# Seven MLP chunks in the partial sum, a tail in quadrants of 112 columns, and the first MLP weights on 112 rows, in a one-token transformer block

## The chip, the cores and the metric

The kernel runs on one core of a Trainium2 chip. The metric is the device time of one execution in microseconds (us). Before the change it is 213.39 us, the median of three runs (213.22 to 213.51).

## What is computed

One decode step of a transformer block for B = 4 tokens of width D = 448: attention over the last 1024 cached positions (16 query heads on 8 cached heads of 256), then a two-layer MLP of width F = 1792, each behind a layer norm, with residuals.

```python
h  = x + attention(layernorm(x), k_cache[:, :, 3072:], v_cache[:, :, 3072:]) @ wo
h2 = h + gelu(layernorm(h) @ w1 + b1) @ w2 + b2
```

All numbers are 32-bit floats. The kernel loads 88.30 MB, nearly all of it keys and values.

## The kernel before, in words

The host packs all inputs into a row of arrays, most of them 128 rows high, and SyncE (SP) loads them in one queue in the order of their use (`load`, L54): `wq0` and `k0`, the arrays `l1` to `l8` of about 8 MB each, then the last pieces `vo`, `v7`, `wo`, `w1`, `w2`. They go into three big SBUF buffers in turn (`slot`, L51), so SP waits until TensorE (PE) is done with an older array before it issues a new one. Each load is shared by 16 DMA engines. PE, SP and ScalarE (ACT) follow the order in which the code is written; VectorE (DVE) and GpSimd (POOL) are ordered by the compiler.

The change lies in the end of the kernel, from the last attention output on. There the batch is folded into **quadrants**: the 128 partitions are four groups of 32, the four tokens stand in the first rows of each group, and group j holds the j-th part of the 448 columns. A row of results is so 128 columns long and not 448. 448 is not four times 128: before the change, the first three quadrants hold 128 columns each, and the fourth holds the last 64 columns twice (`columns`, L235), so that each copy can be turned into 64 rows.

- `accs` (L425) is the output projection so far, all 448 columns. `add_quadrants` (L263) folds it with four matmuls into `last` (L430), and `add_rows` (L437) adds the rest of the projection.
- `h` to `hb` (L462 to L484) are the residual and the layer norm on [128, 128]. `fold` (L111) has a weight of 0.5/D in the fourth quadrant, because its columns count double. `zT` (L481) is the normed row turned by 90 degrees: three chunks of 128 rows, and a fourth that holds the 64 last rows twice.
- `pu` (L489, matmuls in L502) is the first MLP product, `zT` times `w1t`. `w1` is loaded in two DMAs (L402) on 128 rows: chunks 0 and 1 and the half-wide chunk 3 (rows 0 to 63 hold its left half, rows 64 to 127 its right half), then chunk 2. The loop (L498) goes 0, 1, 3, 2; for chunk 3 a matmul uses 64 rows (`w1_part`, L447). In each chunk four matmuls write the four quadrants of `pu`.
- `u` (L508) is GELU of it, `gT` and `gT_last` (L518, L522) hold it turned, as 14 chunks of 128 rows.
- The second product uses `w2`, which is loaded behind `w1` in five DMAs (L403): chunks 0 to 3, 4 to 7, 8 to 10, 11 and 12, and 13. Chunks 0 to 7 (`first = 8`) go into `pa` (L529), one matmul of 448 columns each, on quadrant c % 4. ACT copies `pa` to `pas` (L533). Chunks 8 to 13 go straight into `py` (L540), four matmuls each, one per quadrant. Behind chunk 10, `add_quadrants` adds `pas` to `py`.
- `res` (L546) is `py` plus `hb`; the last DMA stores it (L547).

`keep_warm` (L267) are matmuls on zeros that keep PE's clock up; they compute nothing.

Of the kernel before, what the change touches and what calls it, by code (L numbers as in the profile page):

```python
# [8 lines left out]
F32 = mybir.dt.float32  # L9
BF16 = mybir.dt.bfloat16  # L10
AF = mybir.ActivationFunctionType
ALU = mybir.AluOpType
# [3 lines left out]
B, D = 4, 448  # L16
# [3 lines left out]
F = 1792  # L20
P = 128
H = P // 2
ND = 4
NKC = W // P
NFC = F // P
FQ = F // 4
Q = 32
CACHE = NKC * B * DH
HALF = CACHE // 2
WEIGHTS = 4 * D  # L30
SLOT = CACHE + 2 * WEIGHTS + HALF
COLUMNS = ND * B + 4 + 4 * 4
EPS = 1e-5
SCALE = DH ** -0.5

# [1 line left out]
def block_kernel(ctx: ExitStack, tc, wq0, k0, wq1, l1, l2, l3, l4, l5, l6, l7, l8, vo, v7, wo, w1, w2, out):  # L37
    nc = tc.nc
    const = ctx.enter_context(tc.tile_pool(name="const", bufs=1))
    ring = ctx.enter_context(tc.tile_pool(name="ring", bufs=3))  # L40
    work = ctx.enter_context(tc.tile_pool(name="work", bufs=2))
    once = ctx.enter_context(tc.tile_pool(name="once", bufs=1))
    ps_s = ctx.enter_context(tc.tile_pool(name="ps_s", bufs=2, space=PSUM))
    ps_t = ctx.enter_context(tc.tile_pool(name="ps_t", bufs=2, space=PSUM))
    ps_o = ctx.enter_context(tc.tile_pool(name="ps_o", bufs=1, space=PSUM))
# [5 lines left out]
    def slot(name):  # L51
        return ring.tile([P, SLOT], F32, tag="r", name=name)

    def load(t, at, src, pieces=None):  # L54
        dst = t[:, at : at + src.shape[-1]]
        at = 0
        for n in pieces or (src.shape[-1],):
            nc.sync.dma_start(dst[:, at : at + n], src[:, at : at + n])  # L58
            at += n
        return dst  # L60

    def cut(t, sizes):
        parts, at = [], 0
        for n in sizes:
            parts.append(t[:, at : at + n])
            at += n
        return parts


    def wq_parts(y, t, last=None):  # L70
        parts = [(a, y[:, a, :], slice(0, 512), t[:, a * 512 : (a + 1) * 512]) for a in range(3)]
        if last is not None:
            return parts + [(3, y[:H, 3, :], slice(0, 512), last)]
        for i in range(2):
            parts.append((3, y[:, 3 + i, :], slice(i * 2 * P, (i + 1) * 2 * P), t[:, 3 * 512 :]))
        return parts
# [9 lines left out]
    def output_weights(t):  # L86
        return t.rearrange("p (j e) -> p j e", j=4)
# [9 lines left out]
    sel = const.tile([P, Q], F32, name="sel")  # L97
# [9 lines left out]
    zT = const.tile([P, ND, Q], F32, name="zT")  # L107
# [2 lines left out]

    fold = const.tile([P, 4, Q], F32, name="fold")  # L111
    for j in range(4):
        nc.vector.tensor_scalar_mul(fold[: 3 * Q, j, :], sel[: 3 * Q, :], 1.0 / D)
        nc.vector.tensor_scalar_mul(fold[3 * Q :, j, :], sel[3 * Q :, :], 0.5 / D)
    fold = fold.rearrange("p j q -> p (j q)")
    rows_of = ident.rearrange("p (j q) -> p j q", j=4)[:, :, :B]
    qT = [const.tile([P, 2, B, Q], F32, name=f"qT{i}") for i in range(2)]
    pT = [const.tile([P, NKC // 2, B, Q], F32, name=f"pT{i}") for i in range(2)]
    oT = [const.tile([P, 4, Q], F32, name=f"oT{i}") for i in range(2)]
    gT = const.tile([P, 12, Q], F32, name="gT")  # L120
    gT_last = const.tile([P, 2, Q], F32, name="gT_last")
    idle = const.tile([P, 512], BF16, name="idle")
    nc.vector.memset(idle, 0.0)
    for t in qT + oT + pT + [gT, gT_last]:
        nc.gpsimd.memset(t, 0.0)

    rs = const.tile([P, 2 * P + FQ], F32, name="rs")
    xb, b2b, b1b = rs[:, :P], rs[:, P : 2 * P], rs[:, 2 * P :]


    def column_mean(t, name):
# [46 lines left out]
    def score_tiles(n):  # L178
        return [ps_s.tile([P, 512], F32, tag="s", name=f"s{n}_{h}") for h in range(2)]
# [53 lines left out]


    def columns(t, j):  # L235
        if j < 3:
            return t[:, j * P : (j + 1) * P].rearrange("p (i c) -> p i c", i=2)
        return t[:, None, 3 * P :].to_broadcast([t.shape[0], 2, H])


    def transposed_output(n, po, rec, groups):
# [35 lines left out]


    t = slot("t0")
    wqt, xT, b2T, b1T = cut(load(t, 0, wq0), (WEIGHTS, ND * B, 4, 4 * 4))  # L280
    wqt = wq_parts(yT[0], wqt)
    xT = xT.rearrange("p (a b) -> p a b", a=ND)
    ka, kb, wqt1, k2 = cut(load(t, WEIGHTS + COLUMNS, k0), (HALF, HALF, 3 * 512, HALF))
    for i in range(2):
        nc.sync.dma_start(  # L285
            wq1_last[i * Q : (i + 1) * Q, :], wq1[i].rearrange("e (p c) -> e p c", c=512)[:, :4, :]
        )
    d = work.tile([P, ND, B], F32, tag="d", name="d_x")
# [10 lines left out]

    wide = once.tile([P, 2 * 512], F32, tag="p", name="wide")[:, : 6 * P].rearrange("p (n j q) -> p n j q", n=6, j=4)  # L300
    nc.vector.tensor_copy(
        wide[:, 0].rearrange("p j (r b) -> p j r b", b=B), xT[:, :, None, :].to_broadcast([P, ND, Q // B, B])
    )
    biases = b1T.rearrange("p (c j) -> p c j", j=4)
    nc.vector.tensor_copy(wide[:, 1], b2T[:, :, None].to_broadcast([P, 4, Q]))
# [10 lines left out]
    s = score_tiles(0)  # L316
# [16 lines left out]
    k2, v, wo_a, wo_b = cut(load(slot("l1"), 0, l1), (HALF, CACHE, WEIGHTS, WEIGHTS))  # L333
    scores(s, 1, 1, keys(k2))
    p, rec = softmax(0, s)
# [5 lines left out]
    v, wq_a, wq_b, ka = cut(load(slot("l2"), 0, l2), (CACHE, WEIGHTS, WEIGHTS, HALF))  # L341
# [3 lines left out]
    s = score_tiles(1)  # L345
# [7 lines left out]
    p, rec = softmax(1, s)  # L353
# [4 lines left out]
    v, va, wo_a, wo_b = cut(load(slot("l4"), 0, l4), (CACHE, HALF, WEIGHTS, WEIGHTS))  # L358
# [7 lines left out]
    s = score_tiles(2)  # L366
# [8 lines left out]
    p, rec = softmax(2, s)  # L375
# [6 lines left out]
    vb, v, k2 = cut(load(slot("l7"), 0, l7), (HALF, CACHE, HALF // 2))  # L382
    values(0, chunks(va) + chunks(vb), po, range(2, 4))
    values(1, chunks(v), po)
    s = score_tiles(3)
# [9 lines left out]
    e = [slot(f"te{i}") for i in range(3)]  # L395
    v, wot = cut(load(e[0], 0, vo), (CACHE, 2 * D))
# [2 lines left out]
    rest, wo_last = cut(load(e[0], CACHE + 2 * D, wo), (2 * D, WEIGHTS))  # L399
    wot, rest = (t.rearrange("p (j e) -> p j e", j=2) for t in (wot, rest))  # L400
    wo_last = output_weights(wo_last)
    w1t = cut(load(e[2], 0, w1, (2 * F + F // 2, F)), (F, F, F // 2, F))  # L402
    w2t = cut(load(e[1], CACHE, w2, (4 * D, 4 * D, 3 * D, 2 * D, D)), NFC * (D,))  # L403
    for h in range(2):
        scores(s, 1, h, kt[h])
    p, rec = softmax(3, s)
# [20 lines left out]

    keep_warm(3, warm)
    values(1, vt_last, po_last, alone=True)
    last = ps_s.tile([P, 512], F32, tag="s", name="last")[:, :P]  # L430
    ph = last.rearrange("p (i c) -> p i c", i=2)
    add_quadrants(ph, accs, True)
    keep_warm(1, warm)
    transposed_output(4, po_last, rec, range(1, 2))
# [9 lines left out]
        add_rows(oT[1], wo_last[:, i, :], i, i == 3)  # L444


    def w1_part(a, j):  # L447
        if a < 3:
            return slice(0, P), w1t[3 if a == 2 else a][:, FQ * j : FQ * (j + 1)]
        rows = slice(H * (j // 2), H * (j // 2) + H)  # L450
        return rows, w1t[2][rows, FQ * (j % 2) : FQ * (j % 2 + 1)]


    def row_mean(sums, at, name):
        nc.tensor.matmul(at, fold, sums, start=True, stop=True)
        return at
# [2 lines left out]
        return once.tile([P, 1], F32, tag=name, name=name)  # L459

    keep_warm(1, warm)
    h = once.tile([P, P], F32, tag="h", name="h")  # L462
    hs, ds = stat("hs"), stat("ds")
    squares = once.tile([P, 2], F32, tag="squares", name="squares")
    nc.vector.scalar_tensor_tensor(h, last, 1.0, xb, op0=ALU.mult, op1=ALU.add, accum_out=hs)
    pm = ps_m.tile([P, 2], F32, tag="m", name="pm")
    m = row_mean(hs, pm[:, 0:1], "m")
    keep_warm(2, warm)
    d = once.tile([P, P], F32, tag="dh", name="dh")
    nc.vector.tensor_scalar(d, h, m, None, op0=ALU.subtract, op1=ALU.add, accum_out=ds)  # L470
    pm2 = ps_m.tile([P, 2], F32, tag="m", name="pm2")
    m = row_mean(ds, pm2[:, 0:1], "m2")
    keep_warm(2, warm)
    z = once.tile([P, P], F32, tag="z", name="z")
    nc.vector.tensor_scalar(z, d, m, None, op0=ALU.subtract)
    junk = once.tile([P, P], F32, tag="junk", name="junk")
    nc.scalar.activation(junk, d, AF.Square, accum_out=squares[:, 0:1])
    nc.scalar.activation(junk, z, AF.Square, accum_out=squares[:, 1:2])
    pz = ps_m.tile([P, 4, B], F32, tag="m", name="pz")
    nc.tensor.matmul(pz, z, rows_of, start=True, stop=True)  # L480
    nc.vector.tensor_copy(zT[:, :, :B], pz)  # L481
    hb = once.tile([P, P], F32, tag="hb", name="hb")
    nc.vector.tensor_add(hb, h, b2b)
    keep_warm(2, warm)  # L484

# [1 line left out]
    s = stat("r2")  # L487
    u = once.tile([P, FQ], F32, tag="u", name="u")
    pu = ps_s.tile([P, 512], F32, tag="s", name="pu")[:, :FQ]  # L489
# [5 lines left out]
    rsqrt(s, v2, "r2")  # L495
    nc.vector.tensor_mul(s, s, r1)
    keep_warm(1, warm)
    for a in (0, 1, 3, 2):  # L498
        m = Q if a == 0 else B
        for j in range(4):  # L500
            rows, w = w1_part(a, j)
            nc.tensor.matmul(  # L502
                pu[j * Q : j * Q + m, :], zT[rows, a, :m], w, start=(a == 0), stop=(a == 2),
            )


# [11 lines left out]
    dst = gT.rearrange("p (c j) q -> p c j q", c=3)  # L518
# [3 lines left out]
        nc.scalar.copy(gT_last[rows, :, :B], put_last[rows].rearrange("p (j i) q -> p j i q", i=2)[:, :, i, :])  # L522
    keep_warm(1, warm)

    first = 8
    pa = ps_w.tile([P, D], F32, tag="acc", name="pa")
    for c in range(first):
        j, m = c % 4, Q if c < 4 else B
# [2 lines left out]
        )  # L531
    pas = once.tile([P, D], F32, tag="u", name="pas")
    nc.scalar.copy(pas, pa)  # L533
    py = ps_o.tile([P, 2, H], F32, tag="o", name="py")
    for c in range(first, NFC):
        g = gT[:, c, :] if c < 12 else gT_last[:, c - 12, :]
        for j in range(4):
            m, n = (Q, 2) if c == first else (B, 2 if j < 3 else 1)
            w = columns(w2t[c], j) if n == 2 else w2t[c][:, None, 3 * P :]
            nc.tensor.matmul(  # L540
                py[j * Q : j * Q + m, :n, :], g[:, :m], w, start=(c == first), stop=(c == NFC - 1),
            )
        if c == first + 2:
            add_quadrants(py, pas, False)
    res = once.tile([P, P], F32, tag="res", name="res")
    nc.vector.tensor_add(res, py.rearrange("p i c -> p (i c)"), hb)  # L546
    nc.sync.dma_start(out, res)  # L547


# [77 lines left out]
```

## Time and profile before

| | us |
|---|---|
| median of the runs | 213.39 |
| the profiled execution | 213.37 |
| its span, first to last instruction | 211.6 |
| time outside the span | 1.8 |
| PE busy | 134.4 |
| DVE busy | 27.4 |
| ACT busy | 14.3 |
| POOL busy | 5.0 |
| loaded | 88.30 MB |
| mean rate over the span | 418 GB/s |

The profile's times count from the start of the span. In a timeline a row has the start, the length, the engine, the line, the operation, output<-input, the size and the count; in brackets stands how long the engine had been idle before, and what ended the wait. PEld is PE's loading of weights, which runs beside its matmuls and shows most directly when a matmul's data were there. Several instructions of a kind are merged into one row. `te<-w` is a load of a piece of `w1` or `w2`.

### The profile page before, as it was taken

What the parts mean: (1) busy time and instruction counts of PE and PEld (TensorE: products, weight loads), DVE (VectorE), ACT (ScalarE), POOL (GpSimd) and SP (SyncE); (2) the same over time, 40 slices, a digit from 0 to 9 for tenths busy, and PEclk for the clock granted to TensorE, in tenths of its full rate; (3) what the DMA queues carried; (4) which work ended last, traced back from release to release, by engine and by line L of the source; (5) the groups of instructions that cost most, each with busy time, mean ns of one, the idle gap of its engine ahead of it and who ended that gap; (6) DMA issues with size and microseconds to landing.
All of it is one profiled execution on the core that took longest, in us unless ns stands there. A gap on an engine that the chain in (4) does not pass through costs nothing.

```text
span 211.6 us, 2239 instructions
## 1 busy us (share of the span) xinstructions
PE 134.4 (64%) x976; PEld 46.7 (22%) x976; DVE 27.4 (13%) x135; ACT 14.3 (7%) x34; POOL 5.0 (2%) x17
## 2 busy tenths in 40 slices
PE   0460787369058809844900892397299898888993
PEld 0330021022013302231200220123022332324332
DVE  1510011030001200320000110033002003103210
ACT  2010100020001000200000000012000002010311
POOL 5100000000000000000000000000000000000200
PEclk9999999787859985997975599589979999999999
DMA  8898988999899999999999998999999998999991
GB/s 344 355 481 373 563 384 384 420 540 389 384 444 492 408 387 456 468 408 396 471 444 420 408 516 384 395 469 412 455 412 455 409 440 387 426 401 446 411 409 68
DMA packets 3256, 88.42 MB, mean 418 GB/s; under 512 B 368, under 2 KB 624, under 8 KB 1456
## 3 DMA queue, kind: packets, MB, share of 16 engines
q1 hardware_dynamic: 3248, 88.30, 97.1%
q8 instruction: 7, 0.11, 0.2%
q14 instruction: 1, 0.01, 0.0%
HBM read 88.23 MB, written 0.07 MB: 417 GB/s over the span
## 4 chain that ended last, share of the span: by engine, by line
DMA 73%; PE 19%; another core or an unknown queue 3%; DVE 1%; SPq 1%; ACT 1%; issue 1%; ACTq 0%
DMA l<-l 51%; DMA te<-w 13%; PE po L226 10%; DMA te<-vo 9%; PE s L184 4%; PE acc L257 2%; PE py L540 1%; PE pq L153 1%; PE ppt L212 1%; SPq L285 1%; PE between L269 0%; ACT p L198 0%; SPq L58 0%; DVE mx L192 0%
## 5 line engine op out<-in xcount | busy, mean ns | idle before, releaser
L226 PE MATMUL po<-l,pT 128*32 128x512 f32 x192 | 30.0, 782 | 27.1 <-DMA l<-l 26.9
L184 PE MATMUL s<-l,qT 128*32 128x512 f32 x208 | 30.2, 726 | 18.1 <-DMA l<-l 18.1
L226 PEld LDWEIGHTS po<-l,pT 128*32 128x32 f32 x192 | 7.0, 136 | 46.4 <-issue 24.8
L184 PEld LDWEIGHTS s<-l,qT 128*32 128x32 f32 x208 | 7.3, 130 | 39.2 <-DMA l<-l 20.5
L198 ACT ACTIVATE p<-s,nm 128x512 f32<-128x512 f32 x8 | 5.4, 682 | 123.6 <-DVE nm L194 123.6
L192 DVE TENSOR_REDUCE mx<-s 128x1 f32<-128x512 f32 x8 | 5.5, 691 | 60.8 <-PE s L184 60.8
L243 DVE TENSOR_SCALAR o<-po,rec 128x512 f32<-128x512 f32 x5 | 3.8, 751 | 69.8 <-PE po L226 69.8
L269 PE MATMUL between<-idle 128*32 128x512 bf16 x48 | 11.5, 379 | 0.4 <-DVE pT L218 0.4
L153 PE MATMUL pq<-t,yT 128*32 128x512 f32 (+1 forms) x16 | 3.9, 951 | 9.8 <-DMA t<-k 7.0
L269 PEld LDWEIGHTS <-idle 128*32 128x32 bf16 x70 | 6.4, 96 | 10.9 <-issue 5.7
L184 PE MATMUL s<-t,qT 128*32 128x512 f32 x48 | 7.9, 824 | 0.7 <-DVE qT L176 0.7
L226 PE MATMUL po<-te,pT 128*32 128x512 f32 x64 | 7.3, 595 | 1.0 <-DMA te<-vo 0.8
L269 PE MATMUL warm<-idle 128*32 128x512 bf16 x22 | 6.8, 382 | 0.0
L212 PE MATMUL ppt<-ident,p 128*128 128x128 f32 x32 | 4.9, 288 | 2.2 <-ACT p L198 2.2
L257 PE MATMUL acc<-l,oT 128*32 128x448 f32 x48 | 5.1, 545 | 1.6 <-DVE oT L253 1.6
L167 PE MATMUL pqt<-ident,qs 128*128 128x128 f32 x16 | 3.1, 323 | 4.1 <-ACT qs L163 4.1
L153 PE MATMUL pq<-l,yT 128*32 128x512 f32 (+1 forms) x60 | 5.7, 507 | 0.0
L148 POOL TENSOR_TENSOR r<-ve_r,mhalf 128x1 f32<-128x1 f32 x2 | 1.1, 544 | 188.9 <-DVE ve_r L147 188.9
L212 PEld LDWEIGHTS ppt<-ident,p 128*128 128x128 f32 x32 | 3.5, 143 | 5.0 <-ACT p L198 5.0
L163 ACT COPY qs<-pq 128x512 f32<-128x512 f32 x4 | 2.3, 583 | 31.3 <-PE pq L153 31.3
L133 PE MATMUL pm_x<-t,mean 128*128 128x12 f32 x2 | 0.6, 364 | 5.5 <-DMA t<-wq 5.5
L218 DVE COPY pT<-ppt 128x16 f32<-128x16 f32 x32 | 3.4, 164 | 3.6 <-PE ppt L212 3.6
(115 smaller groups left out, 75.4 us busy)
## 6 DMA issues: line engine op xcount, KB each, us to landing
l<-l SPq DMA_DIRECT2D x6, 7936.0 KB, 43.3
l<-l SPq DMA_DIRECT2D x2, 7168.0 KB
t<-k SPq DMA_DIRECT2D x1, 6912.0 KB, 20.6
te<-vo SPq DMA_DIRECT2D x1, 4544.0 KB, 19.7
te<-v SPq DMA_DIRECT2D x1, 3072.0 KB, 24.3
te<-w SPq DMA_DIRECT2D x3, 896.0 KB, 22.9
te<-w SPq DMA_DIRECT2D x1, 2240.0 KB, 21.2
te<-wo SPq DMA_DIRECT2D x1, 1344.0 KB, 29.1
```

The source lines that it names most:

```text
L153: nc.tensor.matmul(pq[j * Q : (j + 1) * Q, cols], y, w, start=start and cols.start == 0, stop=not start and cols.stop == 512,)
L163: nc.scalar.copy(qs, pq)
L167: nc.tensor.transpose(pt[:, i, :], qs[:, i * P : (i + 1) * P], ident)
L184: nc.tensor.matmul(s[h][b * Q : (b + 1) * Q, :], qT[g][:, c, b, :], kt[:, c - cs.start, b, :], start=(g == 0 and c == 0), stop=(g == 1 and ...
L192: nc.vector.reduce_max(mx[:, h : h + 1], s[h], axis=AX.X)
L198: nc.scalar.activation(p[:, h * 512 : (h + 1) * 512], s[h], AF.Exp, bias=nm, scale=SCALE, accum_out=sums[:, h : h + 1],)
L212: nc.tensor.transpose(pt[:, c, :], p[:, (4 * h + c) * P : (4 * h + c + 1) * P], ident)
L218: nc.vector.tensor_copy(pT[g][:, 2 * h : 2 * h + 2, :, at : at + REP], src[:, :, i, :, 2 * g * REP : (2 * g + 1) * REP],)
L226: nc.tensor.matmul(po[b * Q : (b + 1) * Q], pT[g][:, c, b, :], vt[c][:, :, b, :], start=(c == 0 and (alone or g == 0)), stop=(c == NKC // ...
L243: nc.vector.tensor_scalar_mul(o, po, rec)
L257: nc.tensor.matmul(acc[i * Q : (i + 1) * Q, :], oT[g][:, i, :], wt[:, i, :], start=(n == 0 and g == 0), stop=(n == 3 if i < 2 else n == 2 ...
L269: nc.tensor.matmul(warm[:Q], idle[:, :Q], idle, start=True, stop=True)
```

## The change

The fourfold split of the 448 columns becomes even: each quadrant holds R = 112 columns, none of them twice. `columns` is a plain slice, and all tiles of the tail are [128, 112]. `fold` is 1/D everywhere. `zT` has four chunks of 112 rows. `w1` is packed by the host as four chunks of 112 rows, so that the load writes 112 partitions with rows of 7,168 floats, and not 128 partitions with rows of 6,272; the number of bytes is the same. Its first DMA takes three chunks (5,376 floats of each row, before 4,480), the second the fourth chunk. The half-wide chunk is gone.

In the second MLP product, seven chunks go into `pa`; chunk 7 goes into `py` with the rest, and `add_quadrants` stands right behind chunk 7.

Smaller things: `wq0` gets 16 more columns (x once more, in the new split), which is 8 KB. The output stays [128, 128]; `res` is now a constant tile that POOL clears at the start, and only 112 of its columns are written.

```diff
-COLUMNS = ND * B + 4 + 4 * 4
+R = D // 4
+COLUMNS = 2 * ND * B + 4 + 4 * 4
...
-    dst = t[:, at : at + src.shape[-1]]
+    dst = t[: src.shape[0], at : at + src.shape[-1]]
...
-    nc.vector.tensor_scalar_mul(fold[: 3 * Q, j, :], sel[: 3 * Q, :], 1.0 / D)
-    nc.vector.tensor_scalar_mul(fold[3 * Q :, j, :], sel[3 * Q :, :], 0.5 / D)
+    nc.vector.tensor_scalar_mul(fold[:, j, :], sel, 1.0 / D)
...
-    for t in qT + oT + pT + [gT, gT_last]:
+    res = const.tile([P, P], F32, name="res")
+    for t in qT + oT + pT + [gT, gT_last, res]:
         nc.gpsimd.memset(t, 0.0)
...
     def columns(t, j):
-        if j < 3:
-            return t[:, j * P : (j + 1) * P].rearrange("p (i c) -> p i c", i=2)
-        return t[:, None, 3 * P :].to_broadcast([t.shape[0], 2, H])
+        return t[:, j * R : (j + 1) * R]
...
-    w1t = cut(load(e[2], 0, w1, (2 * F + F // 2, F)), (F, F, F // 2, F))
+    w1t = cut(load(e[2], 0, w1, (3 * F, F)), 4 * (F,))
...
-    for a in (0, 1, 3, 2):
+    for a in range(ND):
         m = Q if a == 0 else B
         for j in range(4):
-            rows, w = w1_part(a, j)
             nc.tensor.matmul(
-                pu[j * Q : j * Q + m, :], zT[rows, a, :m], w, start=(a == 0), stop=(a == 2),
+                pu[j * Q : j * Q + m, :], zT[:R, a, :m], w1t[a][:R, FQ * j : FQ * (j + 1)],
+                start=(a == 0), stop=(a == ND - 1),
             )
...
-    first = 8
+    first = 7
...
-        if c == first + 2:
+        if c == first:
             add_quadrants(py, pas, False)
-    res = once.tile([P, P], F32, tag="res", name="res")
-    nc.vector.tensor_add(res, py.rearrange("p i c -> p (i c)"), hb)
+    nc.vector.tensor_add(res[:, :R], py, hb)
     nc.sync.dma_start(out, res)
...
-    w1 = packed(np.asarray(B_w1))
-    w1 = np.concatenate([w1[:, : 2 * F], w1[:, 3 * F :], w1[:, 2 * F : 3 * F]], axis=1)
+    w1 = np.asarray(B_w1).reshape(4, R, F).transpose(1, 0, 2).reshape(R, 4 * F)
```

How instructions stand in a row shows what moves. First SP's queue from the last piece of the attention's weights on, before the change; `te<-w` at 128x4480 and 128x1792 are the two loads of `w1`, the others those of `w2`:

```order
L58 DMA te_703<-wo 128x2688
L58 DMA te_705<-w 128x4480
L58 DMA te_705<-w 128x1792
L58 DMA te_704<-w 128x1792 x2
L58 DMA te_704<-w 128x1344
L58 DMA te_704<-w 128x896
L58 DMA te_704<-w 128x448
```

The same place after the change:

```order
L59 DMA te_701<-wo 128x2688
L59 DMA te_703<-w 112x5376
L59 DMA te_703<-w 112x1792
L59 DMA te_702<-w 128x1792 x2
L59 DMA te_702<-w 128x1344
L59 DMA te_702<-w 128x896
L59 DMA te_702<-w 128x448
```

Only the shape of the two `w1` loads differs; `w2` stays behind them, as before.

Second, PE from the second MLP product to the end, before the change (`pa` is the partial sum, `py` the quadrants):

```order
L529 MATMUL pa<-te_704,gT 32x448 x4
L529 MATMUL pa<-te_704,gT 4x448 x4
L540 MATMUL py<-te_704,gT 32x128 x4
L540 MATMUL py<-te_704,gT 4x128 x3
L540 MATMUL py<-te_704,gT 4x64
L540 MATMUL py<-te_704,gT 4x128 x3
L540 MATMUL py<-te_704,gT 4x64
L265 MATMUL py<-pas,sel 32x128 x4
L540 MATMUL py<-te_704,gT 4x128 x3
L540 MATMUL py<-te_704,gT 4x64
L540 MATMUL py<-te_704,gT_last 4x128 x3
L540 MATMUL py<-te_704,gT_last 4x64
```

After the change:

```order
L521 MATMUL pa<-te_702,gT 32x448 x4
L521 MATMUL pa<-te_702,gT 4x448 x3
L531 MATMUL py<-te_702,gT 32x112 x4
L264 MATMUL py<-pas,sel 32x112 x4
L531 MATMUL py<-te_702,gT 4x112 x16
L531 MATMUL py<-te_702,gT_last 4x112 x8
```

The four matmuls that add `pas` (L265, now L264) move ahead of chunks 8 to 10, and chunk 7 stands between the partial sum and them.

More of the change, by code (lines that the diff above doesn't have):

```diff
@@ L123, in block_kernel @@
     nc.vector.memset(idle, 0.0)
-    for t in qT + oT + pT + [gT, gT_last]:
+    res = const.tile([P, P], F32, name="res")
+    for t in qT + oT + pT + [gT, gT_last, res]:
         nc.gpsimd.memset(t, 0.0)
     rs = const.tile([P, 2 * P + FQ], F32, name="rs")
-    xb, b2b, b1b = rs[:, :P], rs[:, P : 2 * P], rs[:, 2 * P :]
+    xb, b2b, b1b = rs[:, :R], rs[:, P : P + R], rs[:, 2 * P :]
     def column_mean(t, name):
@@ L279, in block_kernel @@
     t = slot("t0")
-    wqt, xT, b2T, b1T = cut(load(t, 0, wq0), (WEIGHTS, ND * B, 4, 4 * 4))
+    wqt, xT, xR, b2T, b1T = cut(load(t, 0, wq0), (WEIGHTS, ND * B, ND * B, 4, 4 * 4))
     wqt = wq_parts(yT[0], wqt)
@@ L301, in block_kernel @@
     nc.vector.tensor_copy(
-        wide[:, 0].rearrange("p j (r b) -> p j r b", b=B), xT[:, :, None, :].to_broadcast([P, ND, Q // B, B])
+        wide[:, 0].rearrange("p j (r b) -> p j r b", b=B),
+        xR.rearrange("p (a b) -> p a b", a=ND)[:, :, None, :].to_broadcast([P, ND, Q // B, B]),
     )
@@ L429, in block_kernel @@
     values(1, vt_last, po_last, alone=True)
-    last = ps_s.tile([P, 512], F32, tag="s", name="last")[:, :P]
-    ph = last.rearrange("p (i c) -> p i c", i=2)
+    ph = ps_s.tile([P, 512], F32, tag="s", name="ph")[:, :R]
     add_quadrants(ph, accs, True)
@@ L444, in block_kernel @@
         add_rows(oT[1], wo_last[:, i, :], i, i == 3)
[L447 to L451, printed above, removed]
     def row_mean(sums, at, name):
@@ L461, in block_kernel @@
     keep_warm(1, warm)
-    h = once.tile([P, P], F32, tag="h", name="h")
+    h = once.tile([P, R], F32, tag="h", name="h")
     hs, ds = stat("hs"), stat("ds")
     squares = once.tile([P, 2], F32, tag="squares", name="squares")
-    nc.vector.scalar_tensor_tensor(h, last, 1.0, xb, op0=ALU.mult, op1=ALU.add, accum_out=hs)
+    nc.vector.scalar_tensor_tensor(h, ph, 1.0, xb, op0=ALU.mult, op1=ALU.add, accum_out=hs)
     pm = ps_m.tile([P, 2], F32, tag="m", name="pm")
@@ L468, in block_kernel @@
     keep_warm(2, warm)
-    d = once.tile([P, P], F32, tag="dh", name="dh")
+    d = once.tile([P, R], F32, tag="dh", name="dh")
     nc.vector.tensor_scalar(d, h, m, None, op0=ALU.subtract, op1=ALU.add, accum_out=ds)
@@ L473, in block_kernel @@
     keep_warm(2, warm)
-    z = once.tile([P, P], F32, tag="z", name="z")
+    z = once.tile([P, R], F32, tag="z", name="z")
     nc.vector.tensor_scalar(z, d, m, None, op0=ALU.subtract)
-    junk = once.tile([P, P], F32, tag="junk", name="junk")
+    junk = once.tile([P, R], F32, tag="junk", name="junk")
     nc.scalar.activation(junk, d, AF.Square, accum_out=squares[:, 0:1])
@@ L479, in block_kernel @@
     pz = ps_m.tile([P, 4, B], F32, tag="m", name="pz")
-    nc.tensor.matmul(pz, z, rows_of, start=True, stop=True)
-    nc.vector.tensor_copy(zT[:, :, :B], pz)
-    hb = once.tile([P, P], F32, tag="hb", name="hb")
+    nc.tensor.matmul(pz[:R], z, rows_of, start=True, stop=True)
+    nc.vector.tensor_copy(zT[:R, :, :B], pz[:R])
+    hb = once.tile([P, R], F32, tag="hb", name="hb")
     nc.vector.tensor_add(hb, h, b2b)
@@ L533, in block_kernel @@
     nc.scalar.copy(pas, pa)
-    py = ps_o.tile([P, 2, H], F32, tag="o", name="py")
+    py = ps_o.tile([P, 512], F32, tag="o", name="py")[:, :R]
     for c in range(first, NFC):
@@ L537, in block_kernel @@
         for j in range(4):
-            m, n = (Q, 2) if c == first else (B, 2 if j < 3 else 1)
-            w = columns(w2t[c], j) if n == 2 else w2t[c][:, None, 3 * P :]
+            m = Q if c == first else B
             nc.tensor.matmul(
-                py[j * Q : j * Q + m, :n, :], g[:, :m], w, start=(c == first), stop=(c == NFC - 1),
+                py[j * Q : j * Q + m], g[:, :m], columns(w2t[c], j), start=(c == first), stop=(c == NFC - 1),
             )
-        if c == first + 2:
+        if c == first:
             add_quadrants(py, pas, False)
-    res = once.tile([P, P], F32, tag="res", name="res")
-    nc.vector.tensor_add(res, py.rearrange("p i c -> p (i c)"), hb)
+    nc.vector.tensor_add(res[:, :R], py, hb)
     nc.sync.dma_start(out, res)
@@ L604 @@
     w2 = w2.transpose(1, 0, 2).reshape(P, NFC * D)
-    b2 = np.asarray(B_b2)
-    b2 = np.concatenate([b2, b2[3 * P :]]).reshape(ND, P).T
+    xR = np.zeros((P, ND * B), np.float32)
+    xR[:R] = x.reshape(B, 4, R).transpose(2, 1, 0).reshape(R, 4 * B)
+    b2 = np.zeros((P, 4), np.float32)
+    b2[:R] = np.asarray(B_b2).reshape(4, R).T
     b1 = np.zeros((4, 4 * P), np.float32)
@@ L611 @@
     arrays = {
-        "wq0": np.concatenate([wq[0], xT, b2, b1], axis=1), "k0": k0, "wq1": wq1, **loads, "vo": vo, "v7": v[7], "wo": wo_end, "w1": w1, "w2": w2,
+        "wq0": np.concatenate([wq[0], xT, xR, b2, b1], axis=1), "k0": k0, "wq1": wq1, **loads, "vo": vo, "v7": v[7], "wo": wo_end, "w1": w1, "w2": w2,
     }
@@ L625 @@
     got = np.asarray(r.results[0]["out"]).reshape(4, Q, P)[:, :B, :]
-    return np.ascontiguousarray(got.transpose(1, 0, 2).reshape(B, 1, 4 * P)[:, :, :D])
+    return np.ascontiguousarray(got[:, :, :R].transpose(1, 0, 2).reshape(B, 1, D))
```

## Prediction

> **What bounds the kernel now.** I begin with the page: the line of the DMA engines in forty slices, the queues, and the chain that ended last. Then the windows, to see whether a stage differs.
>
> ```profile
> DMA  8898988999899999999999998999999998999991
> q1 hardware_dynamic: 3248, 88.30, 97.1%
> DMA 73%; PE 19%; another core or an unknown queue 3%; DVE 1%; SPq 1%; ACT 1%; issue 1%; ACTq 0%
> ```
>
> ```profile
> core 0: us, PE busy (x) PEld busy (x) DVE busy (x) ACT busy (x) POOL busy (x), PEclk, DMA share, GB/s
> ...
> 50.00:100.00 50.00, 29.80 (x220) 10.39 (x216) 5.22 (x28) 2.51 (x6) 0.00 (x0) 0.84 0.99 427
> 100.00:150.00 50.00, 28.25 (x201) 8.64 (x192) 4.61 (x23) 1.92 (x5) 0.00 (x0) 0.78 1.00 432
> ...
> 190.00:200.00 10.00, 8.99 (x110) 4.49 (x102) 3.10 (x13) 2.09 (x5) 0.94 (x2) 1.00 1.00 427
> ```
>
> The sixteen DMA engines are busy from the start to the last slice, at 427 to 432 GB/s in each window. No stage of the attention sets the end: the loads do, and the order in which PE works matters only behind the last of them. The sizes of the last loads (DMA issues), and PE's weight loads, which show when each piece was there:
>
> ```profile
> te<-w SPq DMA_DIRECT2D x3, 896.0 KB, 22.9
> te<-w SPq DMA_DIRECT2D x1, 2240.0 KB, 21.2
> ...
> te<-w SPq DMA_DIRECT2D x1, 672.0 KB, 26.6
> te<-w SPq DMA_DIRECT2D x1, 448.0 KB, 20.1
> te<-w SPq DMA_DIRECT2D x1, 224.0 KB, 18.2
> ```
>
> ```profile
> 205.18 0.17 PEld L529 LDWEIGHTS pa<-te,gT 128*4 128x4 f32 x8 [0.56 <-DMA te<-w]
> 206.78 0.56 PEld L540 LDWEIGHTS py<-te,gT 128*32 128x32 f32 x24 [1.44 <-DMA te<-w]
> 207.26 0.33 PEld L265 LDWEIGHTS py<-pas,sel 128*32 128x32 f32 x8
> 207.86 0.11 PEld L540 LDWEIGHTS py<-te,gT 128*4 128x4 f32 x8 [0.27 <-DMA te<-w]
> ...
> 208.39 0.11 PEld L540 LDWEIGHTS py<-te,gT_last 128*4 128x4 f32 x8 [0.21 <-DMA te<-w]
> ```
>
> Each of the last four pieces of `w2` is waited for, up to the very last, at 208.39. Between 206.78 and 208.39 came 448 + 224 KB, 688,128 bytes in 1.61 us: 427 GB/s, the rate of the windows. So the time is the moment of the last load plus a short tail: 208.39 to the end of the span at 211.6, and 1.8 us outside it. An edit counts if it moves the last load, or if it stands behind it.
>
> **The change part by part.**
>
> *Behind the last load* stand chunk 13's four matmuls, the sum, and the store.
>
> ```profile
> L540 PE MATMUL py<-te,gT_last x16: 219/272/273, 208.0 to 208.5; 128*4 128x128 f32 x12, 128*4 128x64 f32 x4
> L546 DVE TENSOR_TENSOR res<-py,hb x1: 292/292/292, 208.9 to 208.9; 128x128 f32<-128x128 f32 x1
> L508 DVE SCALAR_TENSOR_TENSOR u<-pu,r,rs x2: 407/446/484, 202.3 to 202.7; 128x256 f32<-128x256 f32 x1, 128x192 f32<-128x192 f32 x1
> ```
>
> A matmul pass of 128 columns takes 272 ns, one of 64 takes 219: 0.83 ns a column. The longest quadrant loses 16 columns in each of its two passes: 2 x 16 x 0.83 = 27 ns. DVE takes 77 ns more for 256 columns than for 192, 1.2 ns a column: 16 columns are 19 ns. Together -0.05 us. The store keeps its size: nothing.
>
> *The order on PE ahead of the last load.* `add_quadrants` now stands ahead of chunks 8 to 13, so these queue behind PE's wait for `pas`.
>
> ```profile
> 206.31 0.53 ACT L533 COPY pas<-pa 128x448 f32<-128x448 f32 x1 [1.54 <-PE pa L529]
> 204.47 1.70 PE L529 MATMUL pa<-te,gT 128*32 128x448 f32 x16
> 206.79 0.75 PE L540 MATMUL py<-te,gT 128*32 128x128 f32 x21 [0.61 <-DMA te<-w]
> ```
>
> Chunk 7's quadrants fit into the 0.61 us in which PE waited. The partial sum ends where it did, since its last four matmuls run side by side in four quadrants, so `pas` is there at 206.84, and PE goes on at about 206.9, 0.1 us later than before. Then come the four adds and chunks 8 to 10. By the weight loads above, 24 for twelve matmuls in 0.48 us and 8 for four in 0.33, that is 0.81 us: PE is ready at 207.7, and chunk 11 comes at 207.86. Cost nothing, with 0.15 us to spare here and 0.21 more before chunk 13.
>
> *The first MLP product.*
>
> ```profile
> 198.68 0.19 PEld L502 LDWEIGHTS pu<-te,zT 128*32 128x32 f32 x8 [0.46 <-DVE ve_r L147]
> 199.09 0.13 PEld L502 LDWEIGHTS pu<-te,zT 128*4 128x4 f32 x4 [0.22 <-issue]
> 199.46 0.13 PEld L502 LDWEIGHTS pu<-te,zT 128*4 128x4 f32 x4 [0.24 <-issue]
> 200.35 0.11 PEld L502 LDWEIGHTS pu<-te,zT 64*4 64x4 f32 x8 [0.76 <-issue]
> 201.21 0.11 PEld L502 LDWEIGHTS pu<-te,zT 128*4 128x4 f32 x8 [0.75 <-DMA te<-w]
> ...
> 198.71 3.44 PE L502 MATMUL pu<-te,zT 128*32 128x448 f32 x32 [0.19 <-DMA te<-w]
> ```
>
> The first load of `w1` grows by 112 KB, so it would land 114,688 / 427,000 = 0.27 us later. Against that, a pass of four matmuls takes 0.37 us (199.09 to 199.46), a chunk 0.75; around the 64-row chunk the steps are 0.89 and 0.86 us (199.46, 200.35, 201.21), so going without it gives back 0.25. They cancel, and the 0.61 us lie behind it anyway. The layer norm's operations on 112 columns end sooner, but PE stood waiting for `w1` at 198.71: nothing.
>
> *At the start*: `wq0` has 8,192 bytes more, 0.02 us at 427 GB/s. POOL's extra clearing and the four `fold` operations that go lie beside loads: nothing.
>
> *`w1` on 112 rows.* 2240 + 896 KB = 3,211,264 bytes, at 427 GB/s 7.52 us, the same bytes before and after. Every big load of this trace has 128 rows, so none shows what 112 cost; I bound it. Sixteen engines carry 200,704 bytes each, at 26.7 GB/s (427 / 16): eight rows of 25,088 bytes before, seven of 28,672 after.
>
> - Lower end, 0: the engines are the limit (share 1.00 in the windows), seven rows each is an even split, and the bytes are the same. A gain is excluded by just that.
> - Middle, +1.07 us: some engine, or some entry into SBUF behind it, still gets eight rows, as it would by the division of 128: 28,672 more bytes at 26.7 GB/s.
> - Upper end, +7.5 us: with 128 rows, each engine may have a group of eight rows to itself. Seven rows each shift the borders, so that two engines write into one group while others lie idle; were it always two, `w1` takes twice 7.52 us.
>
> If sixteen engines fall at random on the 112 / 8 = 14 groups, 14 x (1 - (13/14)^16) = 9.7 are in use, 61% of the rate: 7.52 / 0.61 = 12.4 us, +4.85. I take this value: that the rate stays at 427 to 432 GB/s in every window, whatever the size of a load, looks like a fixed division in which every engine has its own way, and seven rows break it. `w2` has the old shape and follows with the old distance, so the delay of `w1` reaches the end whole.
>
> [...]
>
> Sum, on the profiled execution of 213.37 us: +4.85 + 0.02 - 0.05 gives 218.2. That execution stands 0.02 below the median, which changes nothing.
>
> **The rivals.** A measurement can tell about 0.2%, 0.43 us, from no change.
>
> *The engines alone are the limit.* Sixteen divides 112, every engine gets the same bytes, and nothing behind the engines gets in the way. The DMA share of 0.99 to 1.00 speaks for it, since busy engines explain 427 GB/s without any second limit; against it, these shares say only that a packet was under way. Then 213.37 + 0.02 - 0.05 = 213.3, not slower. It decides if two engines that write neighbouring rows don't slow each other. Chance 0.23.
>
> [...]
>
> *An uneven division without collisions.* Eight of the longer rows on the busiest way: 213.37 + 1.07 - 0.03 = 214.4. For it speaks that eight rows are the unit of 128; against it that seven is the plainer split. Chance 0.27.
>
> *The wait for `pas` takes the place of the load's.* If PE were more than 0.36 us later at `pas` than worked out, all of chunks 8 to 13 would slip past the last load; each us over that is a us. Since the slack was counted from rows, some 0.1 to 0.5 us: 213.5 to 213.8. Chance 0.03.
>
> *Faster.* All tail terms, doubled, are 0.1 us; only the 64-row steps (0.25) on the path as well could come near 0.43. Chance 0.03.
>
> **How the numbers follow.** Collisions have 0.44, with a range of their own from 215.8 (half of the value) to 220.9 (always two). The forecast is theirs, 218.2 us. The range has to take in the rival at 213.3, without which over 0.2 would be left out, and starts at 213.2. It ends at 219.9, above which I leave about 0.1 of the collisions. Faster by over 0.2%: 0.03. Within 0.2%: the first rival, 0.23. Slower: 0.44 + 0.27 + 0.03 = 0.74.
>
> **What would show it.** PE's first weight load for `pu` tells when `w1` is there: before at 198.68. By the engines alone it comes at 198.95, by the uneven division at about 199.8, by collisions at 202 or later; the window that holds `w1` then falls from 427 to about 260 GB/s, while the DMA share stays near 1.00, because the packets take longer. Behind `w1`, the pieces of `w2` should come at the old distances, and PE should wait for chunk 13's weights as it did. If it does not wait there, the slack of the second step was wrong. If the chunks of `pu` keep a step of 0.87 us, the 64 rows were not its cause. The forecast is wrong if the windows around 195 keep 427 GB/s.

## The result, and the profile after

The changed kernel takes 221.58 us (median of five runs, 221.0 to 221.71), 8.2 us more than before (213.39 us in five runs, 213.22 to 213.51): the ratio is 1.0376, with a 95% interval of 1.0358 to 1.0393. The profiled execution took 221.0 us with a span of 219.2. The direction and the place were those of the forecast; at 218.2 with a range up to 219.9 it was too low, so the size was wrong.

The page of the changed kernel, rates in forty slices and the queue:

```profile
DMA  8999899899899999999999999999999999999991
GB/s 334 414 394 532 371 394 533 371 394 524 371 405 521 387 405 487 405 405 490 405 405 475 417 463 407 463 398 450 398 453 395 431 425 416 427 247 221 235 409 59
q1 hardware_dynamic: 3216, 88.31, 97.1%
```

The engines are as busy as before to the last slice, but in slices 36 to 38 they move 221 to 247 GB/s. One window over that stretch:

```profile
core 0: us, PE busy (x) PEld busy (x) DVE busy (x) ACT busy (x) POOL busy (x), PEclk, DMA share, GB/s
...
195.00:208.00 13.00, 8.89 (x80) 4.50 (x79) 2.10 (x11) 2.06 (x5) 1.08 (x2) 0.76 0.98 230
```

230 of 427 GB/s are 54%, at a share of 0.98: the same bytes keep the engines busy for nearly twice as long. Where PE met this, first the last piece of the attention's weights (`wo`) and, at the end, the sum `res`, before and after:

```profile
193.32 1.25 PEld L439 LDWEIGHTS last<-te,oT 128*32 128x32 f32 x48 [0.43 <-DMA te<-wo]
...
208.86 0.29 DVE L546 TENSOR_TENSOR res<-py,hb 128x128 f32<-128x128 f32 x1 [4.50 <-PE py L540]
```

```profile
194.86 1.95 PEld L438 LDWEIGHTS ph<-te,oT 128*32 128x32 f32 x48 [1.98 <-DMA te<-wo]
205.26 0.23 PEld L493 LDWEIGHTS pu<-te,zT 112*32 112x32 f32 x8 [4.38 <-issue]
...
214.89 0.16 PEld L264 LDWEIGHTS py<-pas,sel 128*32 128x32 f32 x8 [0.76 <-ACT pas L525]
215.01 0.78 PEld L531 LDWEIGHTS py<-te,gT 128*4 128x4 f32 x32
215.78 0.40 PEld L531 LDWEIGHTS py<-te,gT_last 128*4 128x4 f32 x16
...
205.29 4.88 PE L493 MATMUL pu<-te,zT 112*32 112x448 f32 x32 [4.11 <-DMA te<-w]
...
216.50 0.27 DVE L536 TENSOR_TENSOR res<-py,hb 128x112 f32<-128x112 f32 x1 [4.13 <-PE py L531]
```

`wo`, a load on 128 rows that the change doesn't touch, came 1.54 us later. The first load of `w1` came 6.6 us later (198.68 to 205.26). Then `pu` took 4.88 us and not 3.44. And PE no longer waits for the last weights: the last rows have no wait for a load, and the only stop is that for `pas`. PE came too late itself. The sum `res` stands at 216.50, 7.64 us later than before, which is the difference of the profiled executions.

How late PE was can be worked out. In windows of 0.05 us, the DMA engines move the last bytes of the loads up to 207.9 us before the change and up to 215.2 after it, 7.3 us later. Where PE waits for the last weights, it goes on some 0.5 us behind these last bytes (208.39 before), and `res` stands 0.47 us after that (208.86). So, as an estimate, the last weights were there at 215.7 us, `res` could have stood at some 216.1, and PE's own lateness is some 0.4 of the 7.64 us.

### The profile page after: what moved, and what is told of

Its sections match the earlier page's. It is cut to its first block, busy times and chain, and to the rows that moved or that the text cites. A ratio compares the mean times of both kernels' runs of the same rounds, so it can differ in the third digit from the quotient of the medians.

```text
span 219.2 us, 2248 instructions
## 1 busy us (share of the span) xinstructions
PE 132.5 (60%) x982; PEld 47.7 (22%) x982; DVE 26.3 (12%) x131; ACT 14.2 (6%) x34; POOL 5.1 (2%) x18
## 4 chain that ended last, share of the span: by engine, by line
DMA 76%; PE 21%; ACT 1%; DVE 1%; issue 0%; SPq 0%; DVEq 0%; ACTq 0%
DMA l<-l 54%; DMA te<-w 13%; PE s L185 12%; DMA t<-k 9%; PE pq L154 3%; PE pu L493 2%; PE warm L413 1%; PE pa L521 1%; PE py L531 1%; PE pqt L168 1%; PE put L506 0%; ACT qs L164 0%; ACT pas L525 0%; DVE u L500 0%; ACT u L501 0%
## 5 line engine op out<-in xcount | busy, mean ns | idle before, releaser
L227 PE MATMUL po<-l,pT 128*32 128x512 f32 x192 | 27.7, 729 | 28.4 <-DMA l<-l 28.3
L185 PE MATMUL s<-l,qT 128*32 128x512 f32 x208 | 29.3, 708 | 21.4 <-DMA l<-l 21.4
L493 PE MATMUL pu<-te,zT 112*4 112x448 f32 (+1 forms) x32 | 4.9, 772 | 4.1 <-DMA te<-w 4.1
L185 PE MATMUL s<-t,qT 128*32 128x512 f32 x48 | 6.9, 732 | 0.7 <-DVE qT L177 0.7
```

The source lines that it names most:

```text
L185: nc.tensor.matmul(s[h][b * Q : (b + 1) * Q, :], qT[g][:, c, b, :], kt[:, c - cs.start, b, :], start=(g == 0 and c == 0), stop=(g == 1 and ...
L227: nc.tensor.matmul(po[b * Q : (b + 1) * Q], pT[g][:, c, b, :], vt[c][:, :, b, :], start=(c == 0 and (alone or g == 0)), stop=(c == NKC // ...
L493: nc.tensor.matmul(pu[j * Q : j * Q + m, :], zT[:R, a, :m], w1t[a][:R, FQ * j : FQ * (j + 1)], start=(a == 0), stop=(a == ND - 1),)
```

## The experiments

In all of them I compare with runs of the kernel before on the same chip, 213.2 to 213.4 us in the median. "Expected" is what was written ahead of each run. The destination theory is the forecast's: with other counts than 128 rows, engines meet at the same entries of SBUF. It is a guess of mine: no trace shows an entry, and the runs can only tell whether the partitions written decide. The source theory is the rival that the longer rows of `w1` in DRAM (28,672 bytes, before 25,088) are slow to read.

**128 rows with zeros (the changed kernel's rows, the old count).**

```diff
+    w1 = np.concatenate([w1, np.zeros((128 - R, 4 * F), np.float32)])
```

> The changed kernel with 16 rows of zeros below w1, so that its two loads write 128 partitions with rows as long as the changed kernel's (28,672 bytes); all the computing stays on 112 rows. It loads 458,752 bytes more, 1.07 us at 427 GB/s. Destination theory (the load is slow because its rows no longer divide into a group for each engine): 213.4 + 1.07 = 214.4 us, and PE's first weight load for pu near 199.7. Source theory (the longer rows in DRAM are slow to read): 221 to 222 us, as the changed kernel or more.

Measured: 214.41 us (214.35 to 215.8), ratio 1.0081 (1.0051 to 1.0111). Rates and weight loads of this run; `w1` is loaded in the first window and up to 201.87 in the second:

```profile
195.00:200.00 5.00, 3.40 (x19) 1.77 (x23) 1.75 (x10) 2.06 (x5) 1.08 (x2) 1.00 0.96 409
200.00:205.00 5.00, 4.70 (x44) 1.96 (x38) 0.97 (x3) 0.69 (x2) 0.00 (x1) 1.00 1.02 423
```

```profile
199.80 0.19 PEld L493 LDWEIGHTS pu<-te,zT 112*32 112x32 f32 x8 [1.72 <-DVE ve_r L148]
...
208.87 0.11 PEld L531 LDWEIGHTS py<-te,gT 128*4 128x4 f32 x8 [0.34 <-DMA te<-w]
...
209.41 0.11 PEld L531 LDWEIGHTS py<-te,gT_last 128*4 128x4 f32 x8 [0.24 <-DMA te<-w]
...
199.84 3.21 PE L493 MATMUL pu<-te,zT 112*32 112x448 f32 x32 [1.45 <-DMA te<-w]
```

409 and 423 GB/s, with 14% more bytes in the load, and the last weights are waited for again. The first weights of `pu` are there at 199.80 (expected 199.7). The row length costs nothing that shows; 16 rows of zeros take 7.2 us off the changed kernel. The source theory falls here as far as the row length goes.

**Halves of 64 rows (the kernel before).** Each `w1` load becomes two:

```diff
-    w1t = cut(load(e[2], 0, w1, (2 * F + F // 2, F)), (F, F, F // 2, F))
+    at = 0
+    for n in (2 * F + F // 2, F):
+        for r in (slice(0, H), slice(H, P)):
+            nc.sync.dma_start(e[2][r, at : at + n], w1[r, at : at + n])
+        at += n
+    w1t = cut(e[2][:, :at], (F, F, F // 2, F))
```

> The kernel before, with each of the two w1 loads cut into one for partitions 0 to 63 and one for 64 to 127; rows, bytes, order and computing stay. Destination theory: 64 rows are half of the groups, so that sixteen engines write into eight at a time; w1 takes twice 7.5 us, 220 to 221 us in all. Source theory: the rows in DRAM are the old ones, 213.4 to 213.8 us. Sixteen divides 64, so that a rule on the number of engines alone also says 213.4.

Measured: 222.01 us in the median of 220.0, 221.82, 222.2 and 223.34; the ratio of 1.0382 (1.0333 to 1.0432) leaves the last of them out. The window over its `w1`:

```profile
195.00:209.00 14.00, 9.86 (x88) 4.63 (x88) 2.16 (x11) 2.09 (x5) 1.08 (x2) 0.78 0.97 217
```

Half the rate (217 of 427 GB/s), on unchanged rows in DRAM, with a number of rows that sixteen divides and the engines as busy as before (0.97). The number of engines alone does not explain it.

**The number of rows as a dose.** In the kernel before, the first `w1` load (128 x 4,480) is cut into loads of 16 rows, of 32 rows, and of 16 rows that go to every eighth partition; for the last, the host puts the rows of each load together in DRAM.

```diff
+    for r in range(0, P, 16):        # or 32
+        nc.sync.dma_start(e[2][r : r + 16, :at], w1[r : r + 16, :at])
...
+    for r in range(8):               # spaced
+        nc.sync.dma_start(e[2][r::8, :at], w1[16 * r : 16 * r + 16, :at])
```

> The kernel before, with its first w1 load (128 rows of 17,920 bytes, 2.29 MB, 5.37 us at 427 GB/s) cut into eight loads of 16 partitions each; nothing else changes. [...] If all that matters is that an engine has no group of its own, sixteen engines crossing at random lose what the changed kernel lost, about half the rate: 218 to 219 us. Sixteen divides 16, so by the number of engines alone 213.4.

> The same with four loads of 32 partitions each. [...] By the number of engines alone 213.4.

> As the run with eight loads of 16 partitions, but each load's 16 rows go to every eighth partition (r, r + 8, and so on) and not to 16 neighbours. The host orders w1 so that each load still reads 16 rows that lie together in DRAM: shapes, engines and reads are those of that run, only the partitions written differ. [...] Source theory, or a price of small row counts: 227 to 229 us, as the 16 neighbours.

Measured: 227.82 us for 16 neighbours (two runs, 226.99 and 228.65), 223.25 for 32 (222.91 and 223.59), 221.51 for 16 spaced (220.75 to 222.68, ratio 1.037, 1.0344 to 1.0396). The windows over these loads, in this order, one kernel each:

```profile
195.00:210.00 15.00, 7.97 (x64) 4.17 (x64) 2.16 (x11) 2.09 (x5) 1.08 (x2) 0.58 0.96 144
```

```profile
195.00:205.00 10.00, 4.97 (x64) 2.94 (x64) 2.17 (x11) 2.09 (x5) 1.08 (x2) 0.98 0.97 203
```

```profile
195.00:205.00 10.00, 4.97 (x64) 2.94 (x64) 2.16 (x11) 2.09 (x5) 1.09 (x2) 0.98 0.98 209
```

Sixteen spaced rows go at 209 GB/s, sixteen neighbours at 144, with the same shapes, number of loads and reads in DRAM: which partitions are written decides. For 32, 64 and 16 spaced rows 203 to 217 were measured, near half of 427; 16 neighbours kept a third. Which partitions stand in each other's way, and why, is not shown. At half the rate the 2.29 MB of this load would take 5.4 us more, an estimate from the 427 GB/s; the loads of 32 cost 9.9, some 4.5 beyond it. Part of that is PE, shown below. The rest is `wo`: the first weights of `pu` came some 2.5 us later than half the rate gives (206.53 against 198.68 + 5.4), and `wo`, which stands ahead of them in the queue, came 2.33 us later than before:

```profile
195.65 1.25 PEld L443 LDWEIGHTS last<-te,oT 128*32 128x32 f32 x48 [2.78 <-DMA te<-wo]
```

**120 rows.**

```diff
+    w1 = np.concatenate([w1, np.zeros((120 - R, 4 * F), np.float32)])
```

> The changed kernel with 8 rows of zeros below w1: 120 partitions, which fifteen engines can share, eight rows each; 229,376 bytes more than on 112. If it was the odd seven rows that shifted the borders, eight rows each are whole groups again, and the load costs only the longer share of each engine, 1.07 us: 214.4. If only 128 rows are divided so that each engine keeps to its own entry, two engines meet at one entry as on 112: w1 takes twice 8.6 us, 222 to 224 us.

Measured: 224.6 us (223.85 to 225.06), ratio 1.0522 (1.0502 to 1.0542), at 211 GB/s over the load:

```profile
195.00:210.00 15.00, 8.23 (x76) 4.42 (x80) 2.10 (x11) 2.06 (x5) 1.09 (x2) 0.73 0.96 211
```

That is a little more than the 222 to 224 us of the second case. Eight rows for each engine, if fifteen share the load, are no help, so it wasn't the odd seven that broke the division: of the row counts tried here (16, 32, 64, 112, 120 and 128), only 128 keeps the rate (409 and 423 GB/s; the others 144 to 230).

**The distance of rows in DRAM.**

```diff
+    w1 = np.concatenate([w1, np.zeros((R, 1024), np.float32)], axis=1)
...
-    w1t = cut(load(e[2], 0, w1, (3 * F, F)), 4 * (F,))
+    w1t = cut(load(e[2], 0, w1[:, : 4 * F], (3 * F, F)), 4 * (F,))
```

> The changed kernel with 4,096 bytes of unused space behind each row of w1 in DRAM (a distance of 32,768 bytes between rows, before 28,672); the loads read and write what they did. Destination theory: no change, 221 to 222 us. Source theory: the distance of rows matters, another time by over 1 us.

Measured: 222.82 us (222.26 to 223.08), 1.2 over the changed kernel, so by the number alone the source theory has a point. The profile says otherwise:

```profile
205.56 5.86 PE L493 MATMUL pu<-te,zT 112*32 112x448 f32 x32 [5.18 <-DMA te<-w]
...
217.76 0.27 DVE L536 TENSOR_TENSOR res<-py,hb 128x112 f32<-128x112 f32 x1 [4.13 <-PE py L531]
```

The first `w1` load was there only 0.3 us later than in the changed kernel (205.53 against 205.26), but `pu` took 5.86 us and not 4.88. These two, 0.27 + 0.98, are the 1.26 by which `res` came later. So in this execution it is PE; for a slower load that leaves 0.3 us, less than the shift between other runs with the same load (below). All four runs with the longer distance are slower than the five of the changed kernel, and the other three have no trace: that the distance costs nothing is not shown beyond this one.

**PE kept warm while it waits.** In the changed kernel, and in the loads of 32 rows (there 24 for 1):

```diff
-    keep_warm(1, warm)
+    keep_warm(20, warm)
     for a in range(ND):
```

> The changed kernel with 20 warming matmuls in place of one ahead of pu, so that PE's clock stays up while it waits for w1. If the part of the loss that is not the loads' (some 0.4 us of 7.6 in the span) is PE's low clock in pu, pu takes 3.2 us and not 4.9, PE waits again for the last weights, and the time falls by 0.4 us, to 221.2. If it is the new order at the partial sum, pu gets faster and the time stays at 221.6.

> The run with loads of 32 partitions, with 24 warming matmuls in place of one ahead of pu. There PE came 1.84 us later than with waits for the last weights. If that is the low clock after the long wait for w1, this part goes: 223.3 - 1.8 = 221.4 us. If it is the loads alone, 223 us as it was.

Measured for the changed kernel: 221.73 us (221.34 to 222.97), no gain. For the loads of 32 rows: 222.07 (221.09 to 222.49), 1.2 less than without, of 1.8 expected. The changed kernel with warming, then the loads of 32 rows without and with it:

```profile
205.93 0.19 PEld L493 LDWEIGHTS pu<-te,zT 112*32 112x32 f32 x8 [1.79 <-issue]
...
216.42 0.11 PEld L531 LDWEIGHTS py<-te,gT_last 128*4 128x4 f32 x8 [0.23 <-DMA te<-w]
...
216.86 0.28 DVE L536 TENSOR_TENSOR res<-py,hb 128x112 f32<-128x112 f32 x1 [4.55 <-PE py L531]
```

```profile
206.53 0.23 PEld L506 LDWEIGHTS pu<-te,zT 128*32 128x32 f32 x8 [5.98 <-issue]
...
206.56 5.70 PE L506 MATMUL pu<-te,zT 128*32 128x448 f32 x32 [5.71 <-DMA te<-w]
...
218.16 0.29 DVE L550 TENSOR_TENSOR res<-py,hb 128x128 f32<-128x128 f32 x1 [3.68 <-PE py L544]
```

```profile
206.51 0.19 PEld L506 LDWEIGHTS pu<-te,zT 128*32 128x32 f32 x8 [0.71 <-issue]
...
206.54 3.44 PE L506 MATMUL pu<-te,zT 128*32 128x448 f32 x32 [0.24 <-DMA te<-w]
...
215.88 0.11 PEld L544 LDWEIGHTS py<-te,gT_last 128*4 128x4 f32 x8 [0.22 <-DMA te<-w]
...
216.35 0.29 DVE L550 TENSOR_TENSOR res<-py,hb 128x128 f32<-128x128 f32 x1 [4.16 <-PE py L544]
```

With 32 rows the picture is clean: `w1` comes at the same time in both, `pu` takes 3.44 us and not 5.70, PE waits for the last weights again, and `res` comes 1.81 us earlier. In the changed kernel warming also brings the wait back (0.23 us at the last weights), but in that execution `w1` itself was 0.67 us later (205.93), so that the time says nothing. It does show what the loads cost alone: here PE waits for the last weights, and they come 8.0 us later than before (216.42 against 208.39). In the changed kernel's own profiled execution the loads ended earlier than that and PE added its 0.4 us. The loads of `w1` shift by more from run to run (205.26 to 205.93 at the first), so the times of the runs can't tell these 0.4 us.

The granted clock over `pu` (third column from the end) was 0.55 after a wait of 4.11 us in the changed kernel, and 0.50 after 5.71 us in the loads of 32 rows:

```profile
205.00:208.00 3.00, 2.71 (x16) 0.76 (x20) 0.00 (x0) 0.00 (x0) 0.00 (x0) 0.55 0.97 239
```

```profile
205.00:210.00 5.00, 3.44 (x20) 0.71 (x24) 0.00 (x0) 0.00 (x0) 0.00 (x0) 0.50 0.99 392
```

It was 1.00 over `pu` before the change, after 0.19 us (198.7 to 202.0), and 1.00 in the loads of 32 rows with warming, after 0.24 us (205 to 210). In the eight traces with a wait of 4.01 to 7.70 us ahead of `pu`, its matmuls kept PE busy for 4.77 to 6.12 us; in the five with 0.19 to 1.46 us, for 3.21 to 3.44.

Waits between these go both ways. After 1.98 us of waiting for `wo`, the next 48 weight loads took 1.95 us in the changed kernel, at a granted clock of 0.56 (194.8 to 197.0); in the changed kernel with warming they took 1.12 after 2.56 us. So in these traces a wait of 4 us and more was followed by a slow `pu` each time, and a shorter one by slow work now and then.

**The partial sum of eight again**, on the run with 128 rows, and on the changed kernel itself.

```diff
-    first = 7
+    first = 8
...
-        if c == first:
+        if c == first + 2:
```

> The run with 128 partitions (zeros below w1), with the partial sum of eight chunks again, its quadrants added behind chunk 10. Both theories: the order on PE has slack ahead of the last loads, so the time is that of the run it is taken from, 214.4 us, within 0.3. If PE's wait for the partial sum costs something on the path, 0.1 to 0.5 us less.

> The changed kernel, still with w1 on 112 rows, with the partial sum of eight chunks again and its quadrants added behind chunk 10. There PE came too late for the last weights and stopped 0.76 us for the partial sum. If that stop is on the path, chunks 8 to 10 fill it as before, the quadrants follow, and the end comes 0.3 to 0.4 us earlier: 221.2 us, with PE waiting for the last weights or nearly so. If PE's low clock in pu is all, 221.6 as it was.

Measured with 128 rows: 214.76 us, ratio 1.0077 (1.0053 to 1.01), against 1.0081 with seven chunks: the same. Its profile ends as that of the run with seven, with PE waiting 0.24 us for the last weights:

```profile
209.62 0.11 PEld L531 LDWEIGHTS py<-te,gT_last 128*4 128x4 f32 x8 [0.24 <-DMA te<-w]
```

Measured with 112 rows: 221.19 us (220.51 to 222.05), ratio 1.0363 (1.0338 to 1.0389); its interval overlaps that of the changed kernel, so the times alone are inconclusive. From the first weights of `pa` to `res`, the changed kernel and this run:

```profile
212.45 0.19 PEld L521 LDWEIGHTS pa<-te,gT 128*32 128x32 f32 x8
...
216.50 0.27 DVE L536 TENSOR_TENSOR res<-py,hb 128x112 f32<-128x112 f32 x1 [4.13 <-PE py L531]
```

```profile
213.83 0.19 PEld L521 LDWEIGHTS pa<-te,gT 128*32 128x32 f32 x8
...
216.28 0.16 PEld L264 LDWEIGHTS py<-pas,sel 128*32 128x32 f32 x8 [0.40 <-ACT pas L525]
...
205.69 5.86 PE L493 MATMUL pu<-te,zT 112*32 112x448 f32 x32 [5.60 <-DMA te<-w]
...
217.32 0.27 DVE L536 TENSOR_TENSOR res<-py,hb 128x112 f32<-128x112 f32 x1 [3.57 <-PE py L531]
```

4.05 us with seven chunks, 3.49 with eight, and in neither a wait for a load in between: where PE is the late one, the new order costs PE 0.56 us, since chunks 8 to 10 no longer fill the time in which ACT copies. In the changed kernel's profiled execution at most the 0.4 us estimated above could have come of it, because the last weights were there no sooner. In the profiled execution with eight chunks the gain was eaten up by `pu`, which took 5.86 us there and not 4.88.

No version here beats the kernel before: the tail on 112 columns has at most 0.05 us to give, and 128 rows for it cost 16 rows of zeros.

## Why the prediction was right in kind and wrong in size

*What bounds the kernel.* Right for the kernel before and wherever PE waits for the last weights (with 128 rows, in halves, with warming). In the changed kernel PE itself was the last, by some 0.4 us, but its lateness came of the late `w1`.

*Behind the last load, -0.05 us.* The sum on 112 columns took 0.27 us and not 0.29. So small a term can't be told in the runs.

*The order on PE, nothing.* Right where the loads come at their old distance, as the two runs with 128 rows show. Wrong in the changed kernel: the step "PE is ready at 207.7" took PE's start at `pu` and its clock as given. There PE was late, and the stop for `pas` stood on the path; its 0.56 us cost the time 0.4 us at most.

*The first product.* The 64-row chunk did cost about 0.25: with 128 rows loaded, `pu` takes 3.21 us, before 3.44. As forecast, nothing comes of it.

*`w1` on 112 rows.* Of the three readings the right one was taken: the partitions written decide, not the engines, the bytes or the length of the rows in DRAM. For 16 rows that is shown (144 against 209 GB/s); that engines meet at an entry is not. For 112 it is inferred from this and from the 128 rows with zeros, since no run wrote the same 112 rows to other partitions. The step that failed is the size of this term. I put +4.85 us (61% of the rate, engines falling at random on 14 groups), where the measured rate is 54%, and left +7.5 as an end that needs "always two". Two things were missing. Random falling was the wrong picture: the kernel before with halves of 64 rows, where by the theory it is always two, ran at 217 GB/s, and 112 rows at 230, nearly the same. And the loss does not begin at `w1`: with it in the queue, the load ahead of it landed later too (`wo`, 1.54 us; with 128 rows PE's weight loads from it ended at 194.50, before at 194.57). Why is not shown. With 54%, `w1` takes 7.52 / 0.54 = 13.9 us, +6.4; with those 1.54, +7.9. Measured were 7.3 us for the loads and 0.4 for PE in the changed kernel's trace, and 8.0 for the loads in the run with warming. That the delay of `w1` reaches the end whole was right: there `res` stands 8.0 us later, too.

*The seven rows.* The reason given, that seven rows shift the borders of groups of eight, is not borne out: 120 rows, eight for each engine if fifteen share them, are as slow (211 GB/s).

*Seen from the rivals.* The engines alone as the limit, and the uneven division at +1.07, are both excluded by the 221.58 us (they gave 213.3 and 214.4), by the halves and by 144 against 209 GB/s. The rival given 0.03, that the wait for `pas` takes the load's place, came true on top of the slower loads in the changed kernel's trace, within its price of 0.1 to 0.5 us; it took the long wait of 4.11 us and the granted clock of 0.55 behind it, which no rival had.

## What to carry to other kernels

Here a load on all 128 partitions was worth even zeros: 16 rows of zeros below a 3.2 MB load made the changed kernel 7.2 us faster. Busy DMA engines were no sign of a full rate, with a share of 0.98 at 230 GB/s and of 1.00 at 427; compare GB/s between windows. And where an edit makes PE wait, look at the granted clock behind the wait: after 5.71 us it was 0.50, and `pu` took 5.70 us; with PE kept busy by warming matmuls it took 3.44.

## What was not expected of the hardware

The variants vary more from run to run than the kernel before, which took 213.02 to 213.45 us in eight runs: loads of 16 spaced rows took 220.75 to 222.68 in four, but the run with 128 rows and zeros, at 409 to 423 GB/s, also took 214.35 to 215.8 in five. So the slow loads are not shown to be the reason. And with slow loads behind it in the same queue, a load landed later itself: `wo` came 1.5 us later ahead of a `w1` on 112 rows, and 2.3 us later ahead of loads of 32.
